# A retention and mixture-of-experts kernel: ranks, scatters, one block's rows and the logits of block pairs take other places

## The chip, the cores and the metric

The kernel runs on 1 core of one Trainium2 chip. The metric is device time in microseconds (us). Engines: PE (TensorE) does matmuls and transpositions into PSUM, DVE (VectorE) and ACT (ScalarE) do elementwise work, POOL (GpSimd) scales and issues indirect DMAs (gathers and scatters), SP (SyncE) issues the plain DMAs, in the order of its queue.

## The reference

Per head, a retention recurrence over 768 positions (4 batches, 8 heads, head dimension 64); its output rows (3072 tokens x 512) go through a mixture of 8 experts, of which each token uses the best one.

```python
for t in range(S):
    state = gamma * state + einsum('bhd,bhe->bhde', k[:, :, t], v[:, :, t])
    y[:, :, t] = scale * einsum('bhd,bhde->bhe', q[:, :, t], state)
x = y.transpose(0, 2, 1, 3).reshape(B * S, H * D)
logits = (x / |x|) @ (emb / |emb|).T / tau
expert_idx = argmax(logits); gate_w = softmax(logits)[expert_idx]
for e in range(E):
    mask = expert_idx == e
    out[mask] = gate_w[mask, None] * (maximum(x[mask] @ w1[e], 0) @ w2[e])
```

## The kernel before, in words

**Stage 1, the blocks.** The 3072 tokens are 12 blocks m of 256. The loop over m (from line 783) writes out by hand the order of every engine's work (a manual schedule: each engine runs its instructions in program order). For a block, PE makes the scores (L381, 32 instructions), DVE masks them (L401), PE adds the products with the state (L445, inter), updates the state with the next block's keys (L415), makes the logits of the block before (logits_products, L492), transposes the next block's keys and queries (L350, L368) and multiplies the masked scores with the values (L445, intra, in two halves). ACT copies the result to yT (take, L464, L467). POOL scales k and q two blocks ahead (L344, L339). DVE transposes yT to rows (L472), and SP writes the rows to xd in DRAM (L479).

**Routing.** Blocks form groups: (0,1,2), (3,4,5), (6,7), (8), (9,10), (11). When the logits of a group are there, sums (L510, PE), choose (L520 to L530, DVE) and add_counts (L548, L550) pick the experts, oh being the one-hot choice and cum the running counts. count (L537 to L541, PE) and ranks (L557 to L561, DVE) give each token its slot. place (L570) scatters, per half block and on POOL, the token's number and logits into the table tbl. For a group whose choice falls in block m, count, ranks and the first scatters come in block m+1, behind its state update; `waiting` and `ready` carry them. For block 8 (the last of the first 2304 tokens) ranks and pad (L586 to L589) stand at the start of block 10, its two scatters behind the masks of block 10.

**Early rows.** Expert 0's first 288 rows come from blocks 0 to 8. In block 10 SP reads their table entries (early_slots, L606) and POOL gathers the rows xge from xd (L600, three gathers). In block 11 PE transposes them (turn_rows, L617), ACT and DVE split them into xh and xl (L624, L625).

**Weights.** A piece of 512 KB comes by SP into raw (load_piece; the four first pieces of expert 0 by four DMAs each, L192), ACT rounds it to whi (L219) and DVE makes the low part wlo (L224). Products are x's high by weight's high, low by high and high by low, so three matmuls per piece of the contraction (L237 first layer, L1055 and L1105 second layer). Pieces 0 and 1 are loaded at the end of block 8, 2 and 3 in block 9, 4 and 5 in block 10 behind the gather.

**The start of expert 0.** `products()` is the list of the first layer's matmuls; `run(n)` issues n of them, with the last block's logits, sums, choice, counts, ranks, scatters and the sorting of the experts by count in between. ACT's hidden copies (L243) and DVE's low halves (L246) follow each eighth. `square` (L278) sums up the squares of xge's rows for the norm. Then xr0, the 128 last rows of expert 0, is cleared (L1113) and gathered, and PE transposes it in the second layer (L1127).

PSUM banks for short uses come in turn from four (`pt_`), so a matmul into one waits for the reader of its last use.

## Time and profile before

| what | value |
|---|---|
| median of 3 runs | 397.76 us (397.32 to 399.26) |
| the profiled execution's own time | 396.75 us |
| its span, first to last instruction | 395.0 us |
| mean granted clock of PE | 0.997 of full speed |
| busy: PE, DVE, ACT, POOL | 384.7, 241.5, 225.6, 151.1 us |

Busy times count an engine's instructions; matmuls are pipelined, so a busy PE may still have holes between them. The chain of waits follows the work back from the last instruction to what released it. The timeline gives instructions in order of time, with idle time before them and its releaser in brackets. "x8" is the number of instructions merged in a row. The 1.75 us between the span and the execution's own time lie outside the first and last instruction.

### The profile page before, as it was taken

How to read it: one execution, taken by the hardware profiler on the slowest of the kernel's cores; microseconds unless marked ns; L12 is line 12 of the kernel's file. 1: busy time of each engine (PE TensorE's matmuls, PEld its weight loads, DVE VectorE, ACT ScalarE, POOL GpSimd, SP SyncE). 2: the span in 40 equal slices, each digit the busy share in tenths (PEclk: the TensorE clock that was granted, in tenths of full speed). 3: DMA queues.
4: the chain of work that ended last, by engine and by line, in shares of the span. 5: the costliest groups of instructions: out<-in, count | busy, mean ns of one | idle time of the engine just before them, and what ended most of it. 6: DMA issues, size and time to landing. Idle time of an engine off the chain costs nothing.

```text
span 395.0 us, 9539 instructions
## 1 busy us (share of the span) xinstructions
PE 384.7 (97%) x3646; PEld 353.9 (90%) x3646; DVE 241.5 (61%) x518; ACT 225.6 (57%) x400; POOL 151.1 (38%) x171
## 2 busy tenths in 40 slices
PE   8999999999999999999999999999999999999992
PEld 4988888888879988999999999999899889999971
DVE  5565766678998569618763862865467437486300
ACT  5687787887937266537345653735755545454420
POOL 2666487788342516024402712510480161001131
PEclk9999999999999999999999999999999999999998
DMA  8999999999479788695969789696889587933121
GB/s 229 271 313 269 273 244 296 247 271 222 109 206 290 232 208 283 195 248 201 311 186 247 268 259 243 211 332 169 247 284 312 144 278 240 211 113 110 47 94 37
DMA packets 88479, 88.39 MB, mean 224 GB/s; under 512 B 10808, under 2 KB 67000, under 8 KB 88424
## 3 DMA queue, kind: packets, MB, share of 16 engines
q1 hardware_dynamic: 83176, 74.60, 67.2%
q0 software_dynamic: 5072, 13.03, 10.0%
q8 instruction: 30, 0.49, 0.5%
q14 instruction: 25, 0.20, 0.2%
q10 hardware_dynamic: 176, 0.07, 0.1%
HBM read 65.01 MB, written 18.79 MB: 212 GB/s over the span
## 4 chain that ended last, share of the span: by engine, by line
PE 91%; DVE 2%; DMA 2%; issue 2%; ACT 0%; POOL 0%; DVEq 0%; POOLq 0%; ACTq 0%
PE pst L237 12%; PE b L237 10%; PE py L1055 8%; PE py L237 8%; PE py L445 8%; PE b L381 6%; PE b L1105 6%; PE b L1055 6%; PE pst L1055 5%; PE py L1105 4%; PE b L350 3%; PE pst L415 3%; PE pst L1105 3%; PE b L368 3%; DMA raw<-in_moe_w_dram 2%
## 5 line engine op out<-in xcount | busy, mean ns | idle before, releaser
L224 DVE TENSOR_TENSOR wlo<-raw,whi 128x1024 fp32r<-128x1024 f32 x64 | 77.8, 1218 | 22.5 <-ACT whi L219 17.2
L1087 POOL DMA_INDIRECT out_dram<-og,si x28 | 29.0, 1037 | 124.4 <-ACT og L1080 58.2
L219 ACT CAST whi<-raw 128x1024 fp32r<-128x1024 f32 x64 | 66.2, 1043 | 6.6 <-DMA raw<-in_moe_w_dram 6.5
L401 DVE TENSOR_TENSOR pm<-b,mask 128x512 f32<-128x512 f32 x48 | 29.8, 684 | 18.3 <-PE b L381 18.3
L600 POOL DMA_INDIRECT xr<-xd,gi x24 | 28.9, 1206 | 17.2 <-DMA raw<-in_moe_w_dram 10.0
L1036 DVE STREAM_TRANSPOSE xt<-xg 128x384 f32<-128x384 f32 (+1 forms) x28 | 15.7, 578 | 32.0 <-DMA xg<-xs 31.9
L237 PE MATMUL pst<-xl,whi 128*128 128x380 f32 (+7 forms) x96 | 32.2, 335 | 0.0
L237 PE MATMUL pst<-xh,whi 128*128 128x380 f32 (+7 forms) x96 | 32.1, 334 | 0.0
L237 PE MATMUL pst<-xh,wlo 128*128 128x380 f32 (+7 forms) x96 | 32.0, 333 | 0.0
L344 POOL TENSOR_TENSOR hl<-wlo,cst 128x512 f32<-128x512 f32 x22 | 22.5, 1043 | 19.8 <-DMA wlo<-in_k_dram 12.8
L1037 ACT CAST xh<-xt 128x408 fp32r<-128x408 f32 (+6 forms) x28 | 14.2, 510 | 25.1 <-DVE xt L1036 24.8
L570 POOL DMA_INDIRECT tbl<-zt,sloti x24 | 23.9, 996 | 11.1 <-issue 4.8
L263 POOL TENSOR_TENSOR r<-r,half 128x4 f32<-128x4 f32 (+1 forms) x9 | 8.9, 993 | 49.5 <-DVE r L262 49.5
L237 PE MATMUL b<-xh,whi 128*128 128x408 f32 (+7 forms) x80 | 26.8, 335 | 0.0
L237 PE MATMUL b<-xl,whi 128*128 128x408 f32 (+7 forms) x80 | 26.7, 334 | 0.0
L237 PE MATMUL b<-xh,wlo 128*128 128x408 f32 (+7 forms) x80 | 26.6, 333 | 0.0
L237 PE MATMUL py<-xh,whi 128*128 128x288 f32 (+7 forms) x80 | 26.4, 329 | 0.0
L237 PE MATMUL py<-xh,wlo 128*128 128x288 f32 (+7 forms) x80 | 26.2, 328 | 0.0
L237 PE MATMUL py<-xl,whi 128*128 128x288 f32 (+7 forms) x80 | 26.2, 327 | 0.0
L243 ACT ACTIVATE hh<-pst 128x380 fp32r<-128x380 f32 (+7 forms) x24 | 11.6, 485 | 24.5 <-PE pst L237 24.4
L381 PE MATMUL b<-qT,kT 64*128 64x128 f32 x384 | 25.3, 279 | 0.0
L381 PEld LDWEIGHTS b<-qT,kT 64*128 64x128 f32 x384 | 22.9, 188 | 1.9 <-issue 1.0
(221 smaller groups left out, 1042.1 us busy)
## 6 DMA issues: line engine op xcount, KB each, us to landing
raw<-in_moe_w_dram SPq DMA_DIRECT2D x60, 512.0 KB, 6.0
whi<-in_q_dram SPq DMA_DIRECT2D x24, 256.0 KB, 3.9
xd<-x SPq DMA_DIRECT2D x48, 128.0 KB, 3.5
wlo<-in_k_dram SPq DMA_DIRECT2D x11, 512.0 KB
xs<-xr SPq DMA_DIRECT2D x6, 768.0 KB
whi<-in_v_dram SPq DMA_DIRECT2D x6, 512.0 KB, 5.7
wlo<-in_v_dram SPq DMA_DIRECT2D x6, 512.0 KB
xg<-xs SPq DMA_DIRECT2D x16, 192.0 KB, 6.5
```

The source lines that it names most:

```text
L219: nc.scalar.copy(out=hv, in_=rv)
L224: eng.tensor_tensor(out=lv, in0=rv, in1=hv.bitcast(F32), op=ALU.subtract)
L237: nc.tensor.matmul(acc[:, :w], a[:, f], x[:, kt, cols], start=(n == 0), stop=(n == 3 * KT - 1))
L344: return eng.tensor_tensor(out=ks_r[:, m % 3, s, h], in0=kin[m % 3][:, h, s], in1=w[:, h], op=ALU.mult)
L381: nc.tensor.matmul(psc[a][:, j], kTs[m][a * D:(a + 1) * D, j, u].rearrange("p s c -> p (s c)"), q_cols(m, a, j, u), start=True, stop=True, ...
L401: o.append(nc.vector.tensor_tensor(out=pm, in0=psc[a], in1=w, op=ALU.mult))
L445: nc.tensor.matmul(pys[m][b][o * D:(o + 1) * D, j], lhsT, rhs, start=first, stop=True, skip_group_check=True)
L570: i = nc.gpsimd.indirect_dma_start(out=tbl[:, :], out_offset=bass.IndirectOffsetOnAxis(ap=sloti[:, n:n + 1], axis=0), in_=zt[:, n], in_off ...
L600: return nc.gpsimd.indirect_dma_start(out=xr[:n, j, :], out_offset=None, in_=xd[:rows_, :], in_offset=bass.IndirectOffsetOnAxis(ap=gi[:n, ...
L1055: nc.tensor.matmul(acc[:, :c], a[:, f], x[:, kt, :c], start=(n == 0), stop=(n == 3 * FT - 1))
L1087: i = nc.gpsimd.indirect_dma_start(out=out[:, :], out_offset=bass.IndirectOffsetOnAxis(ap=si[:n, e, j:j + 1], axis=0), in_=og[:n, j, :], i ...
L1105: nc.tensor.matmul(acc[:s, :], x[:, kt, at], a, start=(n == 0), stop=(n == 3 * FT - 1))
```

## The change

1. The three yT buffers become one tile of three slots (`yring`), so that the logits of two neighbouring blocks can be made by one batch of matmuls, 512 columns wide, with one DVE transposition: blocks 0 and 1 in block 2, 3 and 4 in block 5, 6 and 7 in block 8. The other blocks' logits stay single.
2. count and ranks of a group move from the next block's middle (for block 8: from the start of block 10) to the end of the block of its choice, behind intra. The scatters are dealt out anew: two of group 1's six at the end of block 6, then three and one; all four of group 2 at the end of block 8; the two of block 8 at the end of block 9.
3. In block 9 the rows of block 8 are turned and written ahead of the loads of weight pieces 2 and 3.
4. In block 11 one of the two weight lows moves ahead of the choice, the other behind the split of the early rows, and so do counts, ranks and scatters of group 4.
5. Behind the blocks, the sums of block 11 come after 14 instead of 11 products, and the three squares after all hidden copies of the first layer.

```diff
@@ -52,6 +52,8 @@
 SW = 16
 FILL = 512
 LOADS = (8, 8)
+
+PAIRS = (2, 5, 8)
 STRIDE = 3200
 NOV = (NT - OV + P - 1) // P
 NONE = 2 * NT
@@ -344,6 +346,7 @@
         return eng.tensor_tensor(out=ks_r[:, m % 3, s, h], in0=kin[m % 3][:, h, s], in1=w[:, h], op=ALU.mult)
 
     kTs, qTs, yTs, Ss, pst, tBs = {}, {}, {}, {}, [None, None], {}
+    yring = ap_.tile([P, 3, KT, T2], F32, name="yT", bufs=1)
 
     def turn_k(m, s, ps, js=range(KT)):
         for j in js:
@@ -457,7 +460,7 @@
                 y_product(m, u, j, a, vs[m][:, u, 2 * j + a], pms[a, u][:, j])
 
     def take(m):
-        yTs[m] = ap_.tile([P, KT, T2], F32, name="yT", bufs=3)
+        yTs[m] = yring[:, m % 3]
         y = yTs[m].rearrange("p (i j) (u c) -> p i (j u) c", i=2, u=2)
         at = (slice(0, 4, 2), slice(1, 4, 2)) if m % NCB else (slice(0, 4, 3), slice(1, 3))
         py = [t.rearrange("p (i j) c -> p i j c", i=2) for t in pys[m]]
@@ -486,19 +489,20 @@
     group_of = {m: g for g, ms in enumerate(GROUPS) for m in ms}
     parts = {}
 
-    def logits_products(m):
+    def logits_products(m, n=1):
         ps = pt_()
         for j in range(KT):
-            nc.tensor.matmul(ps[j * Q:(j + 1) * Q, :T2], enT[:, j, :], yTs[m][:, j, :], start=True, stop=True,
-                             skip_group_check=True)
+            nc.tensor.matmul(ps[j * Q:(j + 1) * Q, :n * T2], enT[:, j, :], yring[:, m % 3:m % 3 + n, j, :], start=True,
+                             stop=True, skip_group_check=True)
         return ps
 
-    def logits_rows(m, ps):
+    def logits_rows(m, ps, n=1):
         g = group_of[m]
         if g not in parts:
             parts[g] = ap_.tile([P, max(map(len, GROUPS)), 2, NQ, Q], F32, name="parts")
-        nc.vector.transpose(out=parts[g][:, m - GROUPS[g][0]].rearrange("p u g e -> p (u g) e"),
-                            in_=ps[:, :T2].rearrange("p (g b) -> p g b", b=Q))
+        i = m - GROUPS[g][0]
+        nc.vector.transpose(out=parts[g][:, i:i + n].rearrange("p m u g e -> p (m u g) e"),
+                            in_=ps[:, :n * T2].rearrange("p (g b) -> p g b", b=Q))
 
     def span(g):
         return slice(2 * GROUPS[g][0], 2 * GROUPS[g][-1] + 2)
@@ -764,7 +768,7 @@
 
 
     last_of = {ms[-1]: g for g, ms in enumerate(GROUPS)}
-    waiting, ready = None, []
+    ready = []
 
     def scale_ahead(m, i):
         if m + 2 < NM:
@@ -773,6 +777,10 @@
             for s in range(2):
                 after(scale_q(m + 2, s), i)
 
+    def place_ready(n):
+        place(ready[:n])
+        del ready[:n]
+
     def place_ranks(g):
         pr = count(g)
         run_all(ranks(g, pr))
@@ -783,8 +791,6 @@
     for m in range(NM):
         nxt = m + 1 < NM
         done = last_of.get(m - 1)
-        if m == NM - 2:
-            place_ranks(waiting)
         py_of(m)
         if m == NM - 2:
             first = [split_cast(), split_cast()]
@@ -797,10 +803,6 @@
             o = masks(psc[u] if m == 0 else scores(m, u), u)
             if u == 0:
                 i = o[0]
-        n = 2 if m < 7 else 3 if m < 8 else 4
-        if m == NM - 2:
-            place(ready)
-            del ready[:]
         if m == 0:
             for j in (*load_q(2), load_k(2)):
                 after(j, i)
@@ -812,6 +814,7 @@
         if m == 2:
             nc.gpsimd.tensor_copy(out=zt[:, :, :2].bitcast(I32), in_=C("ids").rearrange("p (n o) -> p n o", o=2))
         if m == NM - 3:
+            rows(m - 1)
             load_piece()
             load_piece()
         if m == NM - 2:
@@ -850,11 +853,12 @@
                 after(nc.sync.dma_start(
                     out=tbl.rearrange("(e s) c -> e (s c)", e=NE)[:, :FILL * SW].rearrange("e (p x) -> e p x", p=P // NE),
                     in_=none), i)
-            if waiting is not None and m < NM - 2:
-                place_ranks(waiting)
-            place(ready[:n])
-            del ready[:n]
-            logits_rows(m - 1, logits_products(m - 1))
+            if m < NM - 3:
+                place_ready(3 if m == 7 else 2)
+            if m in PAIRS:
+                logits_rows(m - 2, logits_products(m - 2, 2), 2)
+            elif m + 1 not in PAIRS:
+                logits_rows(m - 1, logits_products(m - 1))
             if nxt:
                 state_sums(m + 1)
                 if m == NM - 2:
@@ -871,7 +875,8 @@
                     z = sums(done)
                     run_all(choose(done, z))
                     run_all(add_counts(done))
-                rows(m - 1, gathered if m == NM - 2 else None)
+                if m != NM - 3:
+                    rows(m - 1, gathered if m == NM - 2 else None)
                 if m == NM - 2:
                     for low in first:
                         low()
@@ -883,19 +888,18 @@
                     run_all(add_counts(done))
                 intra(m, 0)
                 intra(m, 1)
+                if done is not None:
+                    place_ranks(done)
+                    if m > 3:
+                        place_ready({6: 2, 8: 5}.get(m))
             else:
+                lows[0]()
                 intra(m, 0)
                 z = sums(done)
                 run_all(choose(done, z))
                 run_all(add_counts(done))
-                for low in lows:
-                    low()
                 intra(m, 1)
-                pr = count(done)
                 ps = [turn_rows(xge, EROWS, kt, bank(f"pst{kt}")) for kt in range(2)]
-                run_all(ranks(done, pr))
-                place(range(span(done).start, span(done).stop))
-        waiting = done
         take(m)
         if m < NM - 2:
             spread_v(m + 1, 0)
@@ -909,6 +913,10 @@
         if m == NM - 1:
             for kt in range(KT):
                 rows_T(xge, EROWS, kt, slice(0, EARLY), ps[kt] if kt < 2 else None)
+            lows[1]()
+            pr = count(done)
+            run_all(ranks(done, pr))
+            place(range(span(done).start, span(done).stop))
 
         for _ in range(LOADS.count(m)):
             load_piece()
@@ -943,13 +951,13 @@
     rows(m - 1)
     load_piece()
     load_piece()
-    run(11)
+    run(14)
     low = split_cast()
     z = sums(g)
     run_all(choose(g, z))
     run_all(add_counts(g))
     rows(m)
-    run(21)
+    run(18)
     pr = count(g)
     sort_steps = counting()
     run_all(ranks(g, pr))
@@ -972,13 +980,13 @@
     slots(2)
     run(12)
     split()
-    for j, n in EROWS:
-        square(xge, n, j, j)
     run(12)
     split()
     load_piece()
     load_piece()
     run(DF)
+    for j, n in EROWS:
+        square(xge, n, j, j)
     ctxa.close()
     turn_of[:] = ["b2", "b3"]
```

## Rows read from the trace of the kernel before

**Rows 1.** The page: TensorE's busy time and the chain by engine.

```profile
PE 384.7 (97%) x3646; PEld 353.9 (90%) x3646; DVE 241.5 (61%) x518; ACT 225.6 (57%) x400; POOL 151.1 (38%) x171
...
PE 91%; DVE 2%; DMA 2%; issue 2%; ACT 0%; POOL 0%; DVEq 0%; POOLq 0%; ACTq 0%
```

**Rows 2.** The chain in order of time, blocks 8 to 10: start us, us, what.

```profile
80.63 0.57 PE b L492 x8
...
81.79 0.87 PE b L368 x8
...
85.19 1.99 PE b L381 x32
...
87.78 0.93 PE pst L415 x64
88.92 0.57 PE b L492 x8
...
93.65 2.45 PE b L381 x32
```

**Rows 3.** Timeline of PE, 108 to 113 us: start us, us, engine line op.

```profile
108.59 0.31 PE L617 MATMUL pst<-ident,xge 128*128 128x128 f32 x1
109.33 0.33 PE L617 MATMUL pst<-ident,xge 128*128 128x128 f32 x1 [0.43 <-DMA xge<-xd,tb]
109.94 0.79 PE L617 MATMUL pst<-ident,xge 32*128 32x32 f32 x4 [0.28 <-DMA xge<-xd,tb]
110.66 1.16 PE L617 MATMUL b<-ident,xge 128*128 128x128 f32 x6
...
112.31 0.40 PE L237 MATMUL py<-xh,whi 128*128 128x288 f32 x1
```

**Rows 4.** Timeline of POOL, 87 to 105 us.

```profile
87.15 2.04 POOL L344 TENSOR_TENSOR hl<-wlo,cst 128x512 f32<-128x512 f32 x2 [0.65 <-issue]
...
91.35 1.02 POOL L570 DMA_INDIRECT tbl<-zt,sloti  x1 [0.16 <-DVE s L433]
...
97.79 0.97 POOL L570 DMA_INDIRECT tbl<-zt,sloti  x1 [0.30 <-issue]
104.31 1.06 POOL L600 DMA_INDIRECT xge<-xd,tb  x1 [5.54 <-issue]
```

**Rows 5.** Timeline of SP's DMA queue, 87 to 102 us.

```profile
87.24 9.08 SPq L192 DMA_DIRECT2D raw<-in_moe_w_dram  x16
96.42 3.31 SPq L479 DMA_DIRECT2D xd<-x  x4
101.49 0.39 SPq L606 DMA_DIRECT2D tb<-tbl  x1
```

**Rows 6.** DMA issues from 84 to 155 us: KB each, median us to landing.

```profile
raw<-in_moe_w_dram SPq DMA_DIRECT2D x16, 128.0 KB, 3.3
```

**Rows 7.** Timeline of DVE, 84 to 116 us.

```profile
84.35 0.19 DVE L530 TENSOR_TENSOR oh<-w,wmn 128x32 f16<-128x32 f32 x1
...
108.92 2.36 DVE L224 TENSOR_TENSOR wlo<-raw,whi 128x1024 fp32r<-128x1024 f32 x2
...
113.18 0.44 DVE L500 STREAM_TRANSPOSE parts<-b 128x256 f32<-128x256 f32 x1
...
115.93 0.17 DVE L550 TENSOR_TENSOR cum<-cum,sm 128x8 f16<-128x8 f16 x1
```

**Rows 8.** Timeline of ACT, 123 to 127 us.

```profile
123.86 0.63 ACT L278 ACTIVATE sq<-xge 128x512 bf16<-128x512 f32 x1
...
126.29 1.03 ACT L219 CAST whi<-raw 128x1024 fp32r<-128x1024 f32 x1
```

**Rows 9.** Timeline of PE, 129 to 136 us.

```profile
129.00 0.40 PE L1055 MATMUL pst<-hl,whi 128*128 128x288 f32 x1 [0.52 <-DVE hl L246]
...
135.36 0.60 PE L1127 MATMUL b<-ident,xr 128*128 128x128 f32 x4
```

**Rows 10.** Timeline of POOL, 130 us.

```profile
130.03 1.06 POOL L600 DMA_INDIRECT xr<-xd,tb  x1 [3.25 <-DMA tb<-tbl]
```

## The prediction, made before the changed kernel was run

> **What bounds the kernel now.** I read the page first. TensorE is busy for 97% of the span and the chain that ends last is TensorE for 91% [rows 1]; no other engine gets beyond 61%. So the time is the length of TensorE's work plus the holes in it, and an edit pays only if it shortens that work or closes a hole. The change touches the twelve blocks and the first expert, so I then read the chain in order of time and the timelines of each engine there, looking for holes. There are four places. At the start of block 10 the 32 products of the scores take 2.45 us instead of the 1.99 us of block 9 [rows 2]: a hole of 0.46 us spread over them, where they wait for PSUM banks that ranks and pad still hold. Around 109 us the transpositions of the early gathered rows run from 108.59 to 111.74 us (0.57 us of logits [rows 2] lie between them and the product at 112.31), with two waits for the gather of 0.43 and 0.28 us in sight [rows 3]. At 129.00 us the second layer waits 0.52 us for the low half of the hidden values [rows 9]. And each batch of logits has a fixed part, below. From there to the end the chain is TensorE almost without a break, so what is won by 136 us is kept.
>
> **What sets the early gather.** Followed backwards: the first gather starts at 104.31 [rows 4] when the table read issued at 101.49 has landed, 2.82 us later [rows 5]. That read waited for the last of six scatters, issued at 97.79, 3.70 us before [rows 4, 5]. The six run back to back from 91.35, (97.79 - 91.35)/5 = 1.29 us apart, and GpSimd was busy with the four scalings from 87.15 before that. SP had finished block 8's rows at 96.42 + 3.31 = 99.73 [rows 5], so GpSimd's queue binds and not SP's.
>
> **The change part by part.**
>
> *Pairs of logits.* Three batches of 8 instructions with 256 columns go, three others become 512 wide. A batch takes 0.57 us [rows 2]. Eight transpositions of 128 columns take 0.87 us, 0.85 ns a column [rows 2]; the logits run in four groups of 32 columns side by side, so their streaming is 8 x 256 x 0.85 ns / 4 = 0.435 us and 0.135 us is fixed. A pair should take 0.135 + 0.87 = 1.0 us against 1.14, three of them save 0.4 us. The bounds are nothing (a pair costs two batches) and this 0.4. I take 0.3. VectorE's transposes of the result are merged likewise, off the path. The single ring for yT adds at most waits of ScalarE's copy on readers two blocks old, which are done: nothing, bound 0.1 us a block if the whole ring counts as one, as VectorE's row transposition precedes it in each block.
> [...]
>
> *Ranks at the end of the block.* The five count matmuls cost TensorE 88.92 - 87.78 - 0.93 = 0.21 us where they stand [rows 2]. Moved behind the second half of the products they cost the same if the choice is done: in block 8 oh is ready at 84.54 [rows 7] and the scores of block 9 follow at 85.19 [rows 2], so 0.65 us of cover is there. Net nothing. VectorE's three rank operations then run while it waits for the next scores. In block 9 the ranks no longer stand behind the row transposition, so most of the 0.46 us hole should close; nothing of that reaches the end by itself, since TensorE then waits for the gather that much longer.
>
> *Scatters.* Two of group 1's six move to the end of block 6 and the four of group 2 to the end of block 8, ahead of the scalings for block 11. GpSimd's total does not change; what counts is when it can begin. Before, it was free at 87.15 - 0.65 = 86.50 after three scatters [rows 4]; one is left there, so it is free some 2.6 us sooner, at about 83.9, and the ranks set the start: oh at 84.54, TensorE free at 85.19, less the 0.3 us of the pairs, plus 0.2 for the counts and about 0.6 for the ranks, 85.8. Four scatters to 91.0, four scalings of 4.1 us (87.15 to 91.2 in [rows 4]) to 95.1, two scatters at 95.3 and 96.6. The last is 1.2 us earlier than 97.79. Lower bound nothing (the ranks or GpSimd's gaps eat it), upper 1.2. What is delayed: block 11's k is scaled at 93.1 instead of 89.2, first used in block 10 behind the scores and the first products, after 96; covered by 3 us.
>
> *SP.* Rows of block 8 now stand between weights 0-1 and 2-3. SP issues 16 loads in 9.08 us, 0.57 each [rows 5]: eight to 91.4, rows (their transposition follows the masks of block 9, an estimated 5 us behind its scores' start at 85.19 [rows 2], about 90) to 94.7, eight more to 99.3. The table read can go at 101.49 - 1.2 = 100.3, just behind them. But the eight loads land 3.3 us after issue [rows 6], up to 102.6, and the read shares their queue, so I give back a third: the gather starts **0.8 us earlier**. Rows of block 9, weights 4-7 and all behind the gather move along.
>
> *Block 11.* The transpositions end 0.8 us earlier, at 110.9. The counts were under the wait for the gather and now follow it: **+0.2 us**. First products at 112.31 - 0.8 + 0.2 = 111.7. VectorE's subtractions (xl) are no longer behind 2.36 us of weight lows [rows 7], but one low (1.18 us) and the ranks (some 0.5) now follow them. The last xl needs ScalarE's cast first, about 1 us after its transposition: 111.9; low 113.1; ranks 113.6; parts 114.0. Before, parts ended at 113.18 + 0.44 = 113.62 [rows 7]. The sums now wait for 14 products instead of 11: 47 products lie between 129.00 and 135.36 [rows 9], 0.135 us each, so they are reached at 111.7 + 1.9 = 113.6: **+0.4 us** of waiting; bounds 0 and 0.8. The low of the fourth piece, wanted by the twelfth product at 113.2, is just in time. At product 32 the count needs cum, 116.10 - 113.62 = 2.5 us behind parts [rows 7]: 116.5, and TensorE is there at 113.6 + 0.6 + 18 x 0.135 = 116.6: no wait, by little.
>
> *Squares.* Three of them begin on ScalarE at 123.86, and the cast of the last weight piece follows at 126.29 [rows 8]; VectorE's low and the hidden low follow, and TensorE waits 0.52 us [rows 9]. Issued behind all hidden copies, the squares stand where ScalarE is idle: **-0.5 us**. They delay the clearing of xr0, which stands ahead of its gather; but that gather waits for the table until 130.03 anyway [rows 10], and three squares from about 126 on, at most 2.4 us [rows 8], end before 128.5.
>
> *Sum.* -0.8 + 0.2 + 0.4 - 0.5 = **-0.7 us**. Against the profiled execution that is 396.75 - 0.7 = 396.05; that execution ran 1.0 us below the median of the runs, so against the median 397.76 it is 397.06, **397.1 us**. A measurement of this kernel can tell about 0.5%, 2 us, from no change.
>
> **What is late next.** The gather of xr0 is issued at 130.03 [rows 10] and used at 135.36 [rows 9], 5.3 us; the early gather took 108.59 - 104.31 = 4.3 us to its first use [rows 3, 4]. So there is 1.0 us of slack, and VectorE's chain of sorting, which leads to that gather, does not come sooner. A gain above 1 us would stop here.
>
> **The rivals.**
> *All holes close (0.18).* Nothing waits in block 11, the read lands at once: -1.2 + 0.2 - 0.5, with some more from a wait that I have not seen, -1.5 to -2.2: 396.0, 395.5 at best. For it: the queue times add up to 1.2. Against it: the 1.0 us of slack at xr0.
> *Moved, not removed (0.2).* The gather comes 0.3 us sooner, block 11 gives it back at the sums, the squares pay for the counts: 397.8. For it: TensorE is 97% busy and GpSimd's work is the same. It holds too if the six scatters are bound by something other than GpSimd's order.
> *The table read behind the weights (0.12), slower.* Eight weight loads now stand right ahead of the read instead of block 8's rows. If their queue is served in order and is backed up, the read lands when they have: it decides from a landing past 104.3 on. With twice the median landing, 99.3 + 6.6 = 105.9, the gather is 1.6 us late, and 1.6 + 0.2 + 0.4 - 0.5 = +1.7: 399.5. For it: the loads are issued at 231 GB/s (16 x 128 KB in 9.08 us [rows 5, 6]). Against it: block 8's rows were read back soon after such loads, and the read of before landed in 2.8 us.
> [...]
>
> **How the numbers follow.** The forecast has 0.5. The bounds of its terms (gather 0 to 1.2, sums 0 to 0.8, pairs 0 to 0.4) give 396.2 to 398.3; the best rival reaches 395.5, the slow one 399.5, of which I take in half: 395.5 to 398.8. Faster by over 2 us asks for all the holes and more: 0.12. Slower by over 2 us asks for the slow rival at its worst: 0.04. The rest, 0.84, is within 0.5%.
>
> **What would show it.** Scores of block 10 near 2.0 us; last scatter before the table read some 1 us earlier; table read behind the eight loads of weights, landing within 3.5 us; transpositions of the early rows done near 111; one wait of some 0.4 us at the sums of block 11; no wait at the second layer's hidden low; logits of a pair near 1.0 us. Wrong would be a gather that starts after 104.3, or a new wait of over 1 us anywhere before 150 us.

## The result, and the profile after

| kernel | median (lowest to highest) | profiled execution | its span | granted clock |
|---|---|---|---|---|
| before, 8 runs on the same chip | 397.62 us (396.66 to 399.26) | 396.75 us | 395.0 us | 0.997 |
| changed, 8 runs | 400.75 us (399.32 to 402.83) | 401.56 us | 399.8 us | 0.992 |

The ratio is 1.0078, with a 95% interval of 1.0058 to 1.0098: 3.1 us slower, where 0.7 us faster had been forecast, and outside the range of 395.5 to 398.8 us. L numbers below are those of the changed kernel; the choice is L524 to L534 (L520 to L530 before) and its third step, which writes the tile w, L529 (L525), the ranks' last L565 (L561), the scalings L346 and L341 (L344 and L339), the scatters L574 (L570), the gather L604 (L600).

**Where it is lost.** The stretches of PE come first: windows of the kernel before, then of the changed kernel (window, its length, busy us and instructions of PE, PEld, DVE, ACT, POOL, then granted clock, DMA share, GB/s).

```profile
90.00:95.00 5.00, 5.00 (x77) 4.44 (x75) 4.25 (x18) 3.57 (x7) 4.15 (x5) 1.00 0.79 207
95.00:100.00 5.00, 5.00 (x99) 4.40 (x100) 4.29 (x11) 4.21 (x7) 2.91 (x3) 1.00 1.02 229
```

```profile
90.00:95.00 5.00, 3.61 (x54) 3.17 (x53) 4.16 (x6) 3.55 (x7) 4.92 (x5) 1.00 0.67 188
95.00:100.00 5.00, 4.35 (x51) 4.02 (x54) 3.68 (x14) 3.55 (x5) 1.99 (x2) 0.66 0.89 218
```

Before, PE had no hole here. Now 1.4 and 0.65 us are empty, and the granted clock is 0.66 of full speed in the second window: 1.00 from 95 to 96 us, 0.68 from 96, 0.50 from 97 to 99, 0.62 from 99, and 1.00 again from 100 on. PE's timeline names what it waited for, first two rows of the kernel before for comparison, then the changed kernel from the logits of block 8 to the start of expert 0, in expert 0's second layer and in expert 1's first (idle time before an instruction and its releaser in brackets):

```profile
93.58 2.52 PE L381 MATMUL b<-qT,kT 64*128 64x128 f32 x32
...
97.99 0.64 PE L492 MATMUL b<-yT,enT 128*32 128x256 f32 x8
```

```profile
79.87 1.07 PE L495 MATMUL b<-yT,enT 128*32 128x512 f32 x8
80.87 0.33 PE L353 MATMUL b<-ident,hl 128*128 128x128 f32 x1
...
95.43 0.17 PE L543 MATMUL b<-oh,tri 128*128 128x16 f16 x1 [1.82 <-DVE oh L534]
...
95.84 0.18 PE L590 MATMUL b<-cum,ones 128*128 128x8 f16 x1 [0.22 <-DVE cum L554]
95.95 3.46 PE L384 MATMUL b<-qT,kT 64*128 64x128 f32 x32
...
101.48 0.64 PE L495 MATMUL b<-yT,enT 128*32 128x256 f32 x8
...
112.52 1.05 PE L621 MATMUL pst<-ident,xge 128*128 128x128 f32 x5 [0.46 <-DMA xge<-xd,tb]
...
115.36 0.40 PE L239 MATMUL py<-xh,whi 128*128 128x288 f32 x1
...
117.64 0.26 PE L514 MATMUL b<-parts,cst 128*32 128x16 f32 x8 [0.16 <-DVE parts L504]
...
138.75 0.63 PE L1135 MATMUL b<-ident,xr 128*128 128x128 f32 x4 [0.73 <-issue]
...
156.43 0.45 PE L239 MATMUL pst<-xl,whi 128*128 128x408 f32 x1 [0.29 <-DVE xl L1051]
```

The counts of block 9 wait 1.82 + 0.22 = 2.04 us for the choice. The scores of block 10 behind them start at 95.95 instead of 93.58, 2.37 us late, and take 3.46 us instead of 2.52. (The chain view of [rows 2] puts the same scores of before at 93.65, with 2.45 us.) The products behind them take 1.28 us instead of 1.10, and the logits of block 10 start at 101.48 instead of 97.99: 2.37 + 0.94 + 0.18 = 3.49 us late. Some of it is won back: the first product of expert 0 starts at 115.36 instead of 112.31 [rows 3], +3.05. The late transposition, at 135.36 in [rows 9], starts at 138.75: +3.39, with a new wait of 0.73 us, for which the profile names no releaser.

The spans of the two profiled executions differ by 4.8 us, more than the medians. Another 0.9 us is lost in expert 1's first layer, where the low halves of its rows are waited for: its first product is 3.39 us late (155.19 against 151.80), its thirteenth 4.30 (158.73 against 154.43). The repetition below does not have this, and the rest was not followed.

Why the choice is late stands in VectorE's timeline of the changed kernel:

```profile
92.08 2.89 DVE L529 SCALAR_TENSOR_TENSOR w<-zt,cst 128x16 f32<-128x16 f32 x1
```

An instruction of 16 elements a partition that took 0.17 us in the kernel before (92.06, below) took 2.89. Its row has no idle time with a releaser ahead of it: the 2.89 us are its own duration. It ended at 94.97. POOL's timeline of the changed kernel in the same stretch, and later:

```profile
86.07 0.97 POOL L574 DMA_INDIRECT tbl<-zt,sloti  x1 [1.56 <-DVE sloti L565]
...
89.90 0.97 POOL L574 DMA_INDIRECT tbl<-zt,sloti  x1 [0.30 <-issue]
90.88 2.06 POOL L346 TENSOR_TENSOR hl<-wlo,cst 128x512 f32<-128x512 f32 x2
92.88 2.05 POOL L341 TENSOR_TENSOR hh<-whi,cst 128x512 f32<-128x512 f32 x2
96.55 1.01 POOL L574 DMA_INDIRECT tbl<-zt,sloti  x1 [1.62 <-DVE ex L591]
97.86 0.97 POOL L574 DMA_INDIRECT tbl<-zt,sloti  x1 [0.30 <-issue]
105.59 1.61 POOL L604 DMA_INDIRECT xge<-xd,tb  x1 [6.75 <-issue]
...
117.51 1.05 POOL L574 DMA_INDIRECT tbl<-zt,sloti  x1 [7.55 <-DVE sloti L565]
...
124.93 0.97 POOL L574 DMA_INDIRECT tbl<-zt,sloti  x1 [0.30 <-issue]
...
135.12 1.06 POOL L604 DMA_INDIRECT xr<-xd,tb  x1 [2.46 <-DMA tb<-tbl]
```

POOL's four scalings run from 90.88 to 94.93 and the choice falls among them; w ends 0.04 us after the last. In the kernel before, the scalings ended at 91.2 [rows 4], ahead of the choice. Its VectorE timeline shows the same w beside a scatter, and an instruction beside a scaling that should have been a warning (POOL's row stands behind it):

```profile
89.40 0.80 DVE L561 SCALAR_TENSOR_TENSOR sloti<-wmn,rank 128x4 int32<-128x4 f32 x1
...
92.06 0.17 DVE L525 SCALAR_TENSOR_TENSOR w<-zt,cst 128x16 f32<-128x16 f32 x1
```

```profile
89.15 2.04 POOL L339 TENSOR_TENSOR hh<-whi,cst 128x512 f32<-128x512 f32 x2
```

The ranks' last step took 0.80 us for four elements (0.16 at 111.64, again for four) and ended at 90.20; the first of the two scalings from 89.15 on ended at about 89.15 + 1.02 = 90.17. It was not the only one: at 47.75 the same step took 0.98 us, again beside scalings.

### The profile page after: what moved, and what is told of

The parts are those of the page before. It is cut to its first block, busy times and chain, and to the rows that moved or that the text cites. A ratio compares the mean times of both kernels' runs of the same rounds, so it can differ in the third digit from the quotient of the medians.

```text
span 399.8 us, 9494 instructions
## 1 busy us (share of the span) xinstructions
PE 385.7 (96%) x3622; PEld 354.2 (89%) x3622; DVE 242.9 (61%) x515; ACT 226.3 (57%) x400; POOL 152.6 (38%) x171
## 4 chain that ended last, share of the span: by engine, by line
PE 52%; DMA 9%; issue 5%; DVE 5%; POOL 2%; SPq 1%; ACT 1%; POOLq 0%; DVEq 0%
PE pst L239 10%; PE b L239 9%; PE py L239 8%; PE b L1113 6%; PE py L1063 5%; PE py L1113 4%; PE b L1063 4%; DMA xg<-xs 3%; PE pst L1063 3%; DMA tbl<-zt,sloti 1%; PE pst L1113 1%; DVE wlo L226 1%; DMA xge<-xd,tb 1%; DMA tb<-tbl 1%; DMA xr<-xd,gi 1%
## 5 line engine op out<-in xcount | busy, mean ns | idle before, releaser
L1095 POOL DMA_INDIRECT out_dram<-og,si x28 | 30.7, 1096 | 127.7 <-ACT og L1088 75.9
L604 POOL DMA_INDIRECT xr<-xd,gi x24 | 29.1, 1212 | 17.2 <-ACT sq L280 9.9
L574 POOL DMA_INDIRECT tbl<-zt,sloti x24 | 24.8, 1035 | 17.5 <-DVE sloti L565 10.0
L346 POOL TENSOR_TENSOR hl<-wlo,cst 128x512 f32<-128x512 f32 x22 | 22.6, 1051 | 16.0 <-DMA wlo<-in_k_dram 10.6
L384 PE MATMUL b<-qT,kT 64*128 64x128 f32 x384 | 26.3, 289 | 0.0
L384 PEld LDWEIGHTS b<-qT,kT 64*128 64x128 f32 x384 | 23.9, 197 | 1.3 <-issue 0.7
```

The costliest lines, as they stand in the source:

```text
L346: return eng.tensor_tensor(out=ks_r[:, m % 3, s, h], in0=kin[m % 3][:, h, s], in1=w[:, h], op=ALU.mult)
L384: nc.tensor.matmul(psc[a][:, j], kTs[m][a * D:(a + 1) * D, j, u].rearrange("p s c -> p (s c)"), q_cols(m, a, j, u), start=True, stop=True, ...
L574: i = nc.gpsimd.indirect_dma_start(out=tbl[:, :], out_offset=bass.IndirectOffsetOnAxis(ap=sloti[:, n:n + 1], axis=0), in_=zt[:, n], in_off ...
L604: return nc.gpsimd.indirect_dma_start(out=xr[:n, j, :], out_offset=None, in_=xd[:rows_, :], in_offset=bass.IndirectOffsetOnAxis(ap=gi[:n, ...
L1095: i = nc.gpsimd.indirect_dma_start(out=out[:, :], out_offset=bass.IndirectOffsetOnAxis(ap=si[:n, e, j:j + 1], axis=0), in_=og[:n, j, :], i ...
```

## The experiments

Theory A: VectorE's short instructions with two operands in SBUF are shut out while POOL's scalings run (a guess, from w's 2.89 us beside them); moving the scalings onto the choice costs the wait, and the clock falls behind it (0.66 in the changed kernel). Rival B: VectorE is not held by POOL's operands, and the loss has to do with something else that the new order does, for instance that the counts at the end of the block wait for the choice wherever it stands. Rival C: the loss is in the late group's scatters (block 11) and in transfers behind the weights.

The runs came in five jobs, each on one chip, and chips differ. The first job's chip took 406.03 us for the kernel before, those of the third to fifth 405.2 to 405.9, the second's 397.46. On the slower ones TensorE stands still in other places (last section), so each run is compared with the runs of before of its own job.

**POOL's order and block 11, first job.** e1 puts group 2's scatters behind the scalings again:

```diff
         if m == NM - 3:
+            place_ready(4)
             rows(m - 1)
...
-                        place_ready({6: 2, 8: 5}.get(m))
+                        place_ready({6: 2, 8: 0}.get(m))
```

e2 puts block 11 back; e3 does both:

```diff
-                lows[0]()
                 intra(m, 0)
...
+                for low in lows:
+                    low()
                 intra(m, 1)
+                pr = count(done)
                 ps = [turn_rows(xge, EROWS, kt, bank(f"pst{kt}")) for kt in range(2)]
+                run_all(ranks(done, pr))
+                place(range(span(done).start, span(done).stop))
...
-            lows[1]()
-            pr = count(done)
-            run_all(ranks(done, pr))
-            place(range(span(done).start, span(done).stop))
...
-    run(14)
+    run(11)
...
-    run(18)
+    run(21)
```

e4 leaves POOL's order and gives four of VectorE's instructions one operand in PSUM:

```diff
+        nc.tensor.matmul(ps[:, 256:256 + NE], ident, C("e16"), start=True, stop=True, skip_group_check=True)
+        kept[g] = ps
...
-        w = ap_.tile([P, nb, NE], F32, name="w", bufs=1)
+        w = kept[g][:, 320:320 + nb * NE].rearrange("p (n e) -> p n e", e=NE)
...
-                                       in1=C("e16").unsqueeze(1).broadcast_to([P, nb, NE]), op0=ALU.is_lt, op1=ALU.add)
+                                       in1=kept[g][:, 256:256 + NE].unsqueeze(1).broadcast_to([P, nb, NE]), op0=ALU.is_lt, op1=ALU.add)
...
-        sm = ap_.tile([P, NE], F32, name="sm", bufs=1)
+        sm = kept[g][:, 400:400 + NE]
...
-        nc.vector.tensor_reduce(out=rank[:, r], in_=rs, axis=AX.X, op=ALU.add)
+        nc.vector.tensor_reduce(out=rk, in_=rs, axis=AX.X, op=ALU.add)
```

> The changed kernel with one thing moved: GpSimd issues group 2's four scatters behind the four scalings for block 11, as before, so that the scalings no longer run while VectorE chooses for block 8. Theory A (VectorE's operation with two operands from SBUF, w, stood still while GpSimd was scaling: 2.89 us instead of 0.17): w takes about 0.2 us again, TensorE does not wait for oh at the end of block 9 (1.82 us in the changed kernel), the granted clock does not fall, block 10's scores take 2.0 to 2.5 us, and the time is 2 to 3 us below the changed kernel, near 398. Theory B (the count at the end of the block waits for the choice wherever it stands, GpSimd has no part in it): the wait of some 1.8 us stays and the time is within 0.7 us of the changed kernel's 400.75. Theory C (the later scatters of group 4 hold expert 1's rows back) expects the wait of 0.7 us at the late transposition and of about 1 us at expert 1's first layer to stay in either case.

> The changed kernel with block 11 and the counts of products behind it as before (both lows, count, ranks and scatters of group 4 ahead of the split of the early rows; 11 and 21 products). Theory C (group 4's scatters, 5.4 us later than before where TensorE is 3.05 us later, delay the last two scatters, the table read and so expert 1's rows): the last scatter of all follows the first product of expert 0 by about 7 us again instead of 9.6, no wait at the late transposition (0.73 us) and none at expert 1's first layer, and the time is about 1 us below the changed kernel, near 399.7. Theory A alone expects the wait of 1.8 us at the end of block 9 to stay, and no gain from this edit beyond 0.3 us.

> Both edits of the two kernels above. If A and C together are the whole loss, the pairs, the rows of block 8 ahead of the weights and the later squares are left: TensorE waits neither at the end of block 9 nor at expert 1, and the time is at or below the kernel before: 396.5 to 397.6. If something else in the change costs time, it stays above 398.5.

> The changed kernel with GpSimd's order untouched, so that the scalings run during the choice as they did; but w, oh, the running count and the slot take one operand from PSUM instead of both from SBUF (e16, w, the sums and the rank are put into the bank of the sums, two more matmul instructions a group). Theory A with the two operands from SBUF as the condition: w takes about 0.2 us although GpSimd scales beside it, TensorE does not wait for oh, block 8's scatters are issued near 95 and 96.5 us, and the time falls by 2 to 3.5 us to 397.5 to 398.5. If the choice is slow for another reason (VectorE slowed by GpSimd whatever its operands, or waiting for something that the profile does not name), w still takes over 1 us and the time stays near 400.7.

Ratios: e1 1.0029 [1.0001, 1.0057], e2 1.0044 [1.0014, 1.0074], e3 1.0057 [1.0024, 1.0089], e4 1.0075 [1.0047, 1.0104]. e4 says nothing on operands: on this chip its choice came at 102.5 us, behind the scalings, and w took 0.18 us there. The intervals overlap, and the changed kernel itself was not among the four. The job settles nothing.

**The same on a chip as the first, second job.** c1 is the kernel before, c2 the changed one, c3 is e3's kernel; e6 is c3 with block 11's scalings released by group 2's slots instead of the masks, so that POOL runs them sooner.

```diff
-        nc.vector.scalar_tensor_tensor(out=sloti[:, r], in0=wmn[:, r], scalar=16.0 * STRIDE, in1=rank[:, r],
+        slot_of[g] = nc.vector.scalar_tensor_tensor(out=sloti[:, r], in0=wmn[:, r], scalar=16.0 * STRIDE, in1=rank[:, r],
...
-            scale_ahead(m, i)
+            scale_ahead(m, slot_of[2] if m == NM - 3 else i)
```

> The kernel before, unchanged, profiled on the same chip as the three runs beside it, for the places of its waits there. Every theory expects the ratio to be 1.000 within its interval; theory A expects its choice for block 8 to run beside scatters, not scalings, with w at about 0.2 us.

> The changed kernel, unchanged, on the same chip as the kernels beside it. Theory A: where the choice for block 8 falls into the scalings for block 11, w takes up to 3 us and ends within 0.05 us of the end of a scaling; ratio near 1.008. If the loss were a matter of the chip on which it was first measured, the ratio would be within 0.003 of 1.

> The changed kernel with the scalings ahead of group 2's scatters and block 11 as before, once more beside its controls. Theories A and C together: no w over 0.3 us, no wait for oh at the end of block 9, none at the late transposition, and 2 to 4 us less than the changed kernel beside it: ratio to the kernel before 0.997 to 1.002. If the loss lies in another part (pairs, rows ahead of weights, counts at the end of the block), ratio as that of the changed kernel.

> As the kernel with both edits, and the scalings for block 11 are released by the slots of group 2 at the end of block 8 instead of by the masks of block 9, so that scalings, four scatters and the last two follow each other about 1 us sooner and the choice falls among scatters. Theory A: the last scatter before the table read is issued 1.0 to 1.4 us sooner than in the kernel before, the early gather 0.5 to 1.2 us sooner, and the time is 0.5 to 1.5 us below the kernel before: ratio 0.996 to 0.999. If the gather is bound by the transfers behind the weights instead, the gather starts no sooner and the ratio is that of the kernel with both edits.

| run | median | ratio | span |
|---|---|---|---|
| c1, before | 397.25 us | 0.9997 [0.9979, 1.0014] | 396.2 us |
| c2, changed | 399.85 us | 1.0073 [1.0043, 1.0102] | 399.5 us |
| c3, both put back | 398.72 us | 1.0017 [0.9990, 1.0043] | 396.2 us |
| e6, scalings sooner | 398.61 us | 1.0033 [1.0009, 1.0057] | 398.3 us |

c2 repeats the loss to the row (timelines of VectorE and PE):

```profile
93.69 2.91 DVE L529 SCALAR_TENSOR_TENSOR w<-zt,cst 128x16 f32<-128x16 f32 x1
...
97.06 0.17 PE L543 MATMUL b<-oh,tri 128*128 128x16 f16 x1 [1.85 <-DVE oh L534]
97.58 3.08 PE L384 MATMUL b<-qT,kT 64*128 64x128 f32 x32
...
139.85 0.63 PE L1135 MATMUL b<-ident,xr 128*128 128x128 f32 x4 [0.77 <-issue]
```

Its first product starts at 116.39 against 113.86 in c1, 2.53 us later, and its late transposition 139.85 - 136.58 = 3.27 us later; the spans differ by the same 3.3. Of this, 0.37 us were there before block 9's wait (its counts begin at 95.03, c1's at 94.66). Then 3.5 us are lost up to the logits of block 10 (103.12 against 99.25), as in the trace of the result; 1.3 us of them are back at the first product, mostly because c1 waits 0.99 us for the early gather and c2 does not; and 0.7 us are lost at the late gather.

The lower clock is not in every execution. Of the fifteen of the changed kernel (eight of the result, seven of c2), the five with a mean granted clock of 0.997 took 398.88 to 399.59 us, the ten below it 399.85 to 402.83. So about 2 us of the loss seem to stay without it; none of the five was profiled.

In c3 both waits are gone and w is 0.17 us again. Its counts stand at the end of the block like c2's and wait for nothing (93.57 to 93.66), so their place alone is not the loss. The late transposition is back where c1 has it. But c3 was 1.09 us ahead of c1 at those counts (two traces of the kernel before, the first and c1, lie 1.26 us apart there), so it loses as much behind them, and that loss shows (PE's timeline, then windows with the columns of above):

```profile
92.22 0.17 DVE L529 SCALAR_TENSOR_TENSOR w<-zt,cst 128x16 f32<-128x16 f32 x1
...
93.75 2.06 PE L384 MATMUL b<-qT,kT 64*128 64x128 f32 x32
...
109.85 0.33 PE L621 MATMUL pst<-ident,xge 128*128 128x128 f32 x1 [1.15 <-DMA xge<-xd,tb]
...
114.57 0.44 PE L239 MATMUL py<-xh,whi 128*128 128x288 f32 x1
114.81 0.44 PE L239 MATMUL py<-xl,whi 128*128 128x288 f32 x1
...
136.57 0.60 PE L1136 MATMUL b<-ident,xr 128*128 128x128 f32 x4
```

```profile
112.00:114.00 2.00, 2.00 (x15) 1.33 (x14) 1.88 (x5) 0.65 (x2) 1.69 (x2) 0.67 0.87 194
114.00:116.00 2.00, 2.00 (x17) 1.72 (x15) 0.83 (x2) 0.00 (x0) 1.39 (x3) 0.50 1.03 250
```

TensorE comes to the early rows sooner, waits 1.15 us for the gather, and behind that products run at a granted clock of 0.50, 0.24 us apart instead of 0.13 (c1, at 1.00). Of c3's 12 executions the five with a mean granted clock of 0.990 or more took 395.5 to 397.9 us (median 397.0), the seven below it 398.6 to 399.9. c1's ten lie between 396.1 and 398.0 at clocks of 0.990 to 0.997. So what c3 still lacks goes with the clock; the profiled execution is one of the five, and which of the two causes the other was not tried. The job has no kernel with only one of the two parts put back, so what each is worth in time on such a chip was not measured.

e6 had its last scatter out at 97.17, 0.98 us before c3's 98.15, and the table read still left later: SP's timeline of e6 and PE's.

```profile
96.10 4.46 SPq L194 DMA_DIRECT2D raw<-in_moe_w_dram  x8
102.53 0.38 SPq L612 DMA_DIRECT2D tb<-tbl  x1
```

```profile
110.69 0.33 PE L623 MATMUL pst<-ident,xge 128*128 128x128 f32 x1 [1.08 <-DMA xge<-xd,tb]
```

The read left 102.53 - 97.17 = 5.36 us behind the last scatter, against 3.58 in c3, 3.92 in the changed kernel, 4.14 in c2, and 3.70 [rows 4, 5] and 4.15 (c1) before. Whether the scatters landed later because of the weights was not tried; in this one trace putting them out sooner did not bring the gather sooner (105.77 against 104.91 in c3), which is the second of its two expectations.

**Fillers for the clock, and the parts alone, third job.** g1 is c3 with work for TensorE ahead of the early rows' transposition; g2, g3 and g4 are the kernels of e1, e2 and e4.

```diff
+                spare = pt_()
+                for _ in range(26):
+                    nc.tensor.matmul(spare[:, :P], ones, tri, start=True, stop=True)
                 ps = [turn_rows(xge, EROWS, kt, bank(f"pst{kt}")) for kt in range(2)]
```

> Both repairs as in the third kernel of the second job, and 26 matmuls of 128 columns into a spare bank put on TensorE in block 11, ahead of the transposition of the early rows, so that TensorE is not idle while it waits for the gather. If what the two repairs still lack is the granted clock (0.67 and 0.50 in 112 to 116 us, products 0.24 us apart instead of 0.133), the clock stays at 0.9 or more there, the products are 0.13 us apart, and 1.0 to 1.3 us come back: about 397.4 us, ratio 0.997 to 1.000. If the gather's transfers themselves are what is late, the first products start no sooner and the time is that of the two repairs or more: ratio 1.001 to 1.004.

> The changed kernel with POOL's two pairs of scalings back ahead of group 2's scatters. If the wait of block 9 (VectorE's w beside POOL's scalings) costs about 2 us of the 3, then w takes 0.2 us, the wait for oh at block 9 is under 0.3 us, and the ratio falls from 1.008 to about 1.003; the wait of the late transposition for its rows (0.7 us) and that of expert 1 stay. If the loss lies in the transfers behind the weights alone, the ratio stays at 1.006 to 1.009.

> The changed kernel with block 11's order on POOL as before (the ranks and scatters of the late group not behind the block's choice). If the wait at block 9 is the larger part, it stays (w near 2.9 us, oh waited for 1.8 us) and the ratio is 1.004 to 1.006; the wait of the late transposition is gone and expert 1's rows come 1 to 2 us sooner. If the late group's order is the whole loss, the ratio is 1.000 to 1.002.

> The changed kernel, POOL's order untouched, with one of the two SBUF operands of VectorE's w, oh, sum and rank read from PSUM instead. If VectorE's instructions with two SBUF operands wait for POOL's, w takes about 0.2 us although it runs beside POOL's scalings (91 to 95 us), TensorE does not wait for oh by over 0.3 us, and the ratio is 1.003 to 1.005. If VectorE is held up by anything else that POOL's scalings do, w stays at 2 to 3 us and the ratio at 1.008.

The chip was a slower one (405.21 us): g1 1.0062 [1.0032, 1.0092], g2 1.0054 [1.0022, 1.0085], g3 1.0067 [1.0036, 1.0099], g4 1.0105 [1.0065, 1.0145]. Choice and scalings met in none of them (w 0.17 to 0.18 us), so g4, like e4, says nothing on operands; its 1.0105 and g1's 1.0062 lie above all that was expected.

**With the changed kernel as the mark, fourth job.** h1 is the changed kernel, h2 e1's, h3 e4's, h4 g1's.

> The changed kernel itself, as the mark for the other three. On a chip where the kernel of before takes about 397.5 us: w 2.9 us beside POOL's scalings, oh waited for 1.8 us, ratio 1.007 to 1.010. On a chip where it takes about 405 us: TensorE gets one matmul per 0.7 us for 3 to 5 us between 92 and 100 us, as in the runs of the first and third job; if that hold-up is the changed kernel's own loss there, ratio 1.007 to 1.012; if it only hides the collision on VectorE, 1.004 to 1.006.

> Scalings of block 9 ahead of group 2's scatters, all else as changed. Collision theory: w 0.2 us, no wait for oh over 0.3 us, 1.5 to 2.5 us less than the changed kernel of this job (ratio to before about 1.003 where before is 397.5). If the collision is not what the loss hangs on: the same as the changed kernel.

> POOL's order as changed; w, oh, sum and rank read one operand from PSUM. If VectorE waits for POOL because both operands lie in SBUF: where choice and scalings coincide, w takes 0.2 to 0.3 us and TensorE's wait for oh is under 0.4 us; time 1 to 2 us under the changed kernel's of this job. If any VectorE instruction beside POOL's scalings is held up: w 2 to 3 us and the changed kernel's time.

> Both repairs and 26 filler matmuls ahead of the early rows' transposition. On a chip where before takes about 397.5 us: granted clock 0.9 or more between 110 and 118 us (0.67 and 0.50 without the fillers), products 0.13 us apart, ratio 0.997 to 1.000; if the gather alone decides, 1.001 to 1.004.

Again a slower chip (405.39 us): h1 1.0089 [1.0054, 1.0124], h2 1.0043 [1.0015, 1.0072], h3 1.0104 [1.0070, 1.0137], h4 1.0073 [1.0036, 1.0109]. Here the change costs as much (3.7 us in the medians), and POOL's old order alone gives 409.11 - 406.39 = 2.7 us of it back. But w takes 0.18 us in h1: the collision is not what was lost here. PE's timeline of h1, then PE's and VectorE's of h2, show what was:

```profile
95.86 0.31 PE L418 MATMUL pst<-whi,hl 64*64 64x64 f32 x2 [0.44 <-issue]
97.28 0.28 PE L418 MATMUL pst<-whi,hl 64*64 64x64 f32 x2 [1.11 <-issue]
98.72 1.57 PE L418 MATMUL pst<-whi,hl 64*64 64x64 f32 x44 [1.16 <-issue]
```

```profile
100.94 1.88 PE L384 MATMUL b<-qT,kT 64*128 64x128 f32 x16 [2.01 <-DVE rs L561]
...
100.71 0.17 DVE L561 TENSOR_TENSOR rs<-b,oh 128x16 f32<-128x16 f32 x1 [4.24 <-remote]
```

In h1 TensorE gets two instructions at a time, 1.42 and 1.44 us from start to start, in block 9's state update. In h2 it waits 2.01 us in block 10's scores for VectorE, which itself had stood still for 4.24 us. So h2's gain on these chips supports the order, not theory A's mechanism, and h3 could not test the operands.

**The collision by itself, fifth job.** h5 puts three tests ahead of block 0 of the changed kernel, which needs no luck with the timing: four multiplications of POOL each, and three short VectorE instructions released by the first.

```diff
+    for kind in range(3):
+        nc.gpsimd.tensor_tensor(out=xge[:, 0], in0=xge[:, 2], in1=xge[:, 2], op=ALU.mult)
+        for _ in range(3):
+            nc.gpsimd.tensor_tensor(out=qs_r[:, 2, :, 0], in0=xge[:, 2].rearrange("p (t d) -> p t d", t=8),
+                                    in1=xge[:, 2].rearrange("p (t d) -> p t d", t=8), op=ALU.mult)
+        for j in range(3):
+            if kind < 2:
+                nc.vector.tensor_tensor(out=probe, in0=xge[:, 0, :16],
+                                        in1=probe if kind == 0 else idle[:, :16], op=ALU.add)
+            else:
+                nc.vector.tensor_reduce(out=probe[:, :1], in_=xge[:, 0, :16], axis=AX.X, op=ALU.min)
```

> The disputed cost by itself, ahead of block 0 of the changed kernel: three times four of POOL's 128x512 multiplications (about 1.03 us each), and beside them, released by the first of each four, three short VectorE instructions (128x16): with both operands in SBUF, with one in SBUF and one in PSUM, and with a single operand. If VectorE's instructions with two SBUF operands are shut out while POOL's run, the first of the first three takes 2.5 to 3.1 us and ends within 0.05 us of the end of POOL's fourth, the other two 0.15 to 0.2 us; all of the second and the third three take 0.15 to 0.2 us. If it is one instruction of POOL that is waited for, the first takes about 1 us. If VectorE is slowed by POOL whatever its operands, the second and third three are long too. If there is no such exclusion, all nine take 0.2 us or less.

The view of one tile of h5 (duration in ns, least, median, most) and its timeline:

```profile
L758 DVE TENSOR_TENSOR probe<-xge,probe x3: 174/902/1002, 4.5 to 5.7; 128x16 f32<-128x16 f32 x3
L758 DVE TENSOR_TENSOR probe<-xge,b x3: 170/170/170, 8.7 to 9.1; 128x16 f32<-128x16 f32 x3
L761 DVE TENSOR_REDUCE probe<-xge x3: 170/170/171, 13.0 to 13.4; 128x1 f32<-128x16 f32 x3
```

```profile
4.40 1.03 POOL L754 TENSOR_TENSOR hh<-xge 128x512 f32<-128x512 f32 x1
4.47 1.00 DVE L758 TENSOR_TENSOR probe<-xge,probe 128x16 f32<-128x16 f32 x1 [1.64 <-POOL xge L752]
...
5.51 1.07 POOL L754 TENSOR_TENSOR hh<-xge 128x512 f32<-128x512 f32 x1
5.71 0.90 DVE L758 TENSOR_TENSOR probe<-xge,probe 128x16 f32<-128x16 f32 x1
```

With both operands in SBUF the instruction starts 0.07 us behind POOL's and ends 0.04 us after it: 1.00 and 0.90 us for 0.17 us of work. The second of the three started in the 0.08 us between two of POOL's and took 0.17. With one operand in PSUM, or a single operand, all six take 0.17 us beside the same work of POOL. That is the exclusion of theory A, in one execution, and it hangs on VectorE's having two operands in SBUF; B falls. Its size is not theory A's: the expected 2.5 to 3.1 us did not come, but the 1 us of the branch in which one of POOL's instructions is waited for. In the changed kernel w sat through the rest of one and two whole ones more. Had each instruction waited for one, w would have ended near 92.95 and oh, which also has two SBUF operands, behind the third scaling near 93.95 instead of 95.38, an estimate from POOL's rows. So some 1.4 of the 2.04 us rest on a repetition that h5 does not show; for it stand the traces of the changed kernel and of c2, where w ends with the fourth scaling.

h6, g1's kernel for the third time:

> Both repairs and 26 filler matmuls ahead of the early rows' transposition, as before. On a chip where before takes about 397.5 us: granted clock 0.9 or more between 110 and 118 us, products 0.13 us apart, ratio 0.997 to 1.000; if the gather alone decides, 1.001 to 1.004. On a chip where it takes about 405 us: 1.006, as twice before.

1.0029 [1.0004, 1.0053] on a chip of 405.86 us. On the slower chips c3's kernel without fillers had 1.0057 (e3) and with them 1.0062, 1.0073 and 1.0029: no difference that can be told. In e3's trace the granted clock is 1.00 from 108 to 124 us without fillers, so there was nothing for them to save. Whether fillers would save the clock on a chip like the first stays open. No kernel here was faster than the one before.

## Why the prediction was wrong, point by point

*The step that failed* is in "Scatters": "GpSimd's total does not change; what counts is when it can begin", and with it "What is delayed: block 11's k is scaled at 93.1 instead of 89.2 ... covered by 3 us". The times were right: four scatters from 85.8 to 91.0 and scalings to 95.1 were forecast, 86.07 to 90.87 and 94.93 came. But I asked only who needs the scaled k, not who shares something with the scalings while they run. At 91.64 to 93.06 VectorE makes the choice, and PE's counts now stood right behind it. Priced at nothing, this cost 2.04 us of waiting on TensorE, and the scores started 2.37 us late. Behind the wait, at the lower clock, they took 0.94 us longer and the products after them 0.18: 3.49 us. (Against the 2.06 us that c3 shows for these scores the forecast gain of the hole is lost as well.) By the first product 0.44 us are back: the counts have left the middle of block 11, and the wait for the gather shrank from 0.71 [rows 3] to 0.46 us, while the counts cost 0.2 us further on. Both signs of being wrong that the prediction names came: a gather after 104.3 (105.59) and a new wait of over 1 us (1.82). In front of me lay [rows 4] and, unread, the 0.80 us of the ranks' last step. In h5, with two operands in SBUF beside POOL's, 0.17 us became 1.00; the 2.89 us of w, through more than one of POOL's instructions, no probe showed by itself.

*Late next.* "The gather of xr0 ... 1.0 us of slack" took its start at 130.03 [rows 10] for fixed. I wrote that one low and the ranks of group 4 now follow the split, and never carried that on to its scatters: the first left at 117.51 and the last at 124.93, 5.4 and 5.5 us later than the 112.08 and 119.46 of the kernel before, while TensorE was 3.05 us later. So the table was read late and the gather came at 135.12, 5.1 us later, 3.6 us ahead of its use instead of 5.3, and the late transposition waited 0.73 us. That this wait is for the gather is read from these times, as the profile names no releaser. Putting block 11 and the scalings back together removed both waits (c3).

*Ranks.* The cover was worked out for block 8, where it holds: the counts take 0.21 us there (84.86 to 85.07), as much as before. In block 9 it was gone, as oh was late. That the 0.46 us hole of block 10 [rows 2] closes is right: 2.06 us in c3.

*Table read and gather.* Forecast 0.8 us sooner; it came at 105.59, 1.3 us later than [rows 4], the table read at 101.78 instead of 100.3. The last scatter stood at 97.86 instead of the 96.6 forecast, since its ranks waited for the choice. From the read to the gather it took 3.81 us instead of 2.82 (3.07 in c2, 2.80 in c1). The slow rival, "the table read behind the weights", asked for a landing past 104.3: it happened in this small form, and in e6 sooner scatters bought nothing there.

*Pairs.* 1.00 us a batch (79.87 to 80.87), as forecast. Against twice 0.57 [rows 2] that is 0.14 us saved.

*Block 11.* +0.2 for the counts came (114.58 to 114.79). The sums waited 0.16 us, not 0.4.

*Squares.* Right: no wait for the second layer's hidden low is left in the changed kernel, and the 0.52 us of [rows 9] are saved (c1 had 0.19 us of the same wait). The clearing of xr0 came later than the forecast allowed: in c3 it starts at 130.56 instead of before 128.5, and the gather of xr0 waits for it (131.38), but TensorE does not.

*The rivals.* "Moved, not removed" at 397.8 is nearest to what c3 gives. That kernel lacks two parts of the change, so it bears the rival out only in part. None of the three had two engines that collide, and the only slow one was sized at 1.7 us.

## What to carry to other kernels

Before an instruction is moved along an engine's queue, write down what every other engine does in the stretch where it lands, not only who waits for its result: here VectorE's instructions with two SBUF operands stood still beside GpSimd's multiplications (0.16 to 0.17 us became 0.80 to 2.91). The ranks' last step in the trace of before, 0.80 us instead of 0.16 and ending with GpSimd's instruction, was the price list for this move. And follow a moved step to its last consumer, through scatters, table read and gather, before a slack is called fixed.

## What the runs showed of the hardware

A VectorE instruction of 0.17 us was held for 2.89 and 2.91 us through three of GpSimd's instructions in a row (changed kernel, c2), but for one only in h5, and for one only in the ranks' last step of the kernel before (0.80 us there and in c1), although the scalings beside it followed each other without a gap as in the changed kernel. Why VectorE gets its turn in one case and not in the other was not found.

A wait of 1.15 us on TensorE was followed by 0.50 of the granted clock in c3, one of 0.72 us in c1 by 1.00.

Chips differ by 2%: the kernel before takes 397.5 us on the chips of the result and of the second job, and 405 to 406 us on the four others. On one of those TensorE goes on by two instructions each 1.42 to 1.44 us from 95.86 to 98.72 us in h1, and VectorE stands still for 4.24 us up to 100.71 us in h2, with "remote" as the releaser, in or just behind a row of four scatters of GpSimd (92.98 to 97.78 in h1, 94.97 to 99.80 in h2); beside the same four scatters of the changed kernel on the result's chip (86.07 to 90.87 us) TensorE has no hole. No profile of the kernel before was taken on the slower chips, and what holds the engines there was not tried.
